# Three more scalings and one copy on ScalarE, one constant added by VectorE, wider weight sums, and a new instruction order in a Winograd residual block

## The chip, the cores and the metric

The kernel runs on one core of a Trainium2 chip. The metric is the device time of one execution in microseconds (us). A profile was taken of one execution; its time stands with the others below. The engines are called as in the profile: PE is TensorE (matmuls; PEld is its weight load), DVE is VectorE, ACT is ScalarE, POOL is GpSimd, SP is SyncE, which here only issues DMAs. Each engine runs its own instructions strictly in the order in which the program lists them and waits for the others by semaphores.

## The reference

Two images (`B = 2`) of 512 channels and 64 x 64 pixels in bf16 go through a residual block: group normalisation in four groups of 128 channels, silu, a 3 x 3 convolution of 512 to 512 channels, an embedding added per channel, and all of it once more:

```python
h = conv3(_silu(gn(x, g1, be1)), w1)
emb = _silu(t_emb) @ w_emb
h = h + emb.reshape(B, C, 1, 1)
h = conv3(_silu(gn(h, g2, be2)), w2)
return x + h
```

## The kernel before

**The arithmetic.** The convolution is done in Winograd form. A tile of rows is turned into combinations of rows (`v_block`, on DVE and ACT), the weights into the matching combinations (`u_blocks`, after transposes on PE), PE multiplies the two and accumulates over channels and taps, and the products are combined into output rows (`one_set`). The row form makes positions 0 to 5 out of four output rows. Positions 0 and 5, and in some chunks also 1 and 3, are computed with a second, column-wise form (`col_pair`, `more_cols`), which costs fewer matmuls and more work on DVE and ACT.

**Tiles and loops.** Channels stand on the 128 partitions, so there are four channel blocks `ct` in and four `ot` out. There are two layers and four chunks of 32 image rows (`chunks`, `idx` 0 to 3: image 0 upper and lower, image 1 upper and lower). For every layer, chunk and `ot`, `one_set` issues the matmuls of a set and the combining work. Between chunks, `v_block(layer, b, ch, c0, n, ...)` prepares a later chunk for two channel blocks at once (`n = 2`; one at a time for the very first chunk). The V buffers alternate between two chunks. The matmuls write three PSUM tiles `acc` in turn, and two more PSUM tiles `xa`, `xb` serve transposes and lone row positions; a tile is free for new matmuls when ACT or DVE has read it.

**Order.** Nothing is issued as the loops run. Every instruction is recorded in a plan (`plan.add`) with its engine, an assumed cost (`vcost` for DVE, `c` in `act`, `cost=` in `pool`) and what it reads and writes. `_Plan.issue` then runs a list scheduler on these costs, forwards and backwards, perturbs the priorities in stages with the random seeds of `STEPS` (L31 to L40), and emits the last order. `FIRST` (L30) is the assumed time to a DMA's first byte. So any change of a cost, of `FIRST` or of `STEPS` gives another order on all engines. All DVE additions go through `tt` (line L330 in the profile), scalings with a constant through `ts` (L335, with two constants L337), all ACT work but the transposes' copies (L531) and two others through `act` (L360).

**Places that the change touches.**
- `STEPS`, `FIRST` (L30 to L40), the assumed costs in `vcost` (L323), `act` (L350) and the power on POOL in `norm` (L458, L459).
- `norm`: mean and variance of a group become scale and shift. Where the statistics come through a PSUM tile (`ps`), DVE already adds epsilon; otherwise POOL adds it (L455) and then raises to the power -1/2 (L458).
- `u_more` (L487), once per `ot` and pair of channel blocks after chunk 0 of layer 1, makes the weights for the column form of positions 1 and 3: two DVE sums, a doubling `ts(g(1), g(1), 2.0)` on DVE (L493), and a third DVE sum.
- `v_block`: first a factor 4 (L658, by ACT in layer 1 and by DVE in layer 0, through `scaled`), then sums. For a chunk in column form, even and odd columns are pulled apart (L683 to L688): for chunks of `ACT_SPLIT` DVE adds in place and ACT makes the copy that pulls apart, for the others DVE adds and pulls apart in one instruction.
- `u_blocks`: six weight sums of 384 elements for each block of 128 input channels (L549 to L554), or, with `wide=True`, three sums of twice the size (L542 to L545), for which the middle tap goes to a scratch tile. Layer 1 uses the wide form with `tmp2`, the upper half of the tile `aux`; layer 0 uses the narrow one (L1071).

Of the kernel before, what the change touches and what calls it, by code (L numbers as in the profile page):

```python
# [11 lines left out]
ACT = mybir.ActivationFunctionType  # L12
ALU = mybir.AluOpType
# [11 lines left out]
class _Plan:  # L25
# [1 line left out]

    LOOK = {"PE": 0.0, "DVE": 0.25, "ACT": 0.6, "POOL": 0.0, "SP": 0.0}
    RATE = 0.36e6
    FIRST = 2.2  # L30
    STEPS = ((0, 3), (300001, 3), (300002, 3), (300003, 2), (300004, 3), (300006, 3), (300007, 3), (300008, 2),  # L31
# [9 lines left out]
    NOISE = 6.0  # L41

    def __init__(self):
# [149 lines left out]
def kernel(  # L193
# [13 lines left out]
    nc = tc.nc  # L207
# [15 lines left out]
    EPS = 1e-5  # L223
# [9 lines left out]
    DVE_SUMS = (1,)  # L233
    COL0 = (1, 2, 3)
    LONE = 1
    ACT_SPLIT = (1, 2, 3)
    MORE = 1
    DSTEP = (TR * P, CQ)
    SLOT = (1, 3, 2, 4, 0, 5)
    assert C % P == 0 and E % P == 0 and C // 4 == P and H % CR == 0 and NFREE == 512  # L240
# [40 lines left out]
    tmp2 = aux[:, CR * W:2 * CR * W]  # L281
# [25 lines left out]
    def size(a):  # L307
        n = 1
        for d in list(a.ap)[1:]:
            n *= d[1]  # L310
        return n
# [5 lines left out]
    def vcost(kind, aps):  # L317
        n = max(size(a) for a in aps)
        if n <= 16:
            return 0.08  # L320
        fast = all(packed(a) for a in aps)
        if kind == "tt":
            return 0.08 + n * (0.00051 if fast else 0.00102)  # L323
        if kind == "ts":
            return 0.07 + n * (0.00026 if fast else 0.00102)
        return 0.08 + n * 0.00104
# [5 lines left out]
    def ts(out, in_, c, op=ALU.mult, c2=None, op1=None, more=(), **kw):  # L332
        def emit():
            if op1 is None:
                nc.vector.tensor_scalar(out=out, in0=in_, scalar1=c, scalar2=None, op0=op)  # L335
            else:
                nc.vector.tensor_scalar(out=out, in0=in_, scalar1=c, scalar2=c2, op0=op, op1=op1)  # L337
        plan.add("DVE", vcost("ts", (out, in_)), emit, [in_] + list(more), [out], **kw)
# [8 lines left out]
    def act(out, in_, func=None, scale=1.0, bias=None, accum=None, **kw):  # L347
        fn = func or ACT.Copy
        ps = in_.tensor.name in psum
        c = size(in_) * (0.00093 if fn == ACT.Silu else 0.00081 if ps else 0.00084) + 0.09  # L350
        if accum is not None:
            c += 0.08

        def emit():
            extra = {}
            if bias is not None:
                extra["bias"] = bias
            if accum is not None:
                extra["accum_out"] = accum
            nc.scalar.activation(out=out, in_=in_, func=fn, scale=scale, **extra)  # L360
        reads = [in_] + [a for a in (scale, bias) if a is not None and not isinstance(a, float)]
        plan.add("ACT", kw.pop("cost", c), emit, reads, [out] + ([] if accum is None else [accum]), **kw)

    def scaled(out, in_, c, on_act):
        if on_act:
            act(out, in_, scale=c)
        else:
            ts(out, in_, c)
# [13 lines left out]
    def pool(emit, reads, writes, cost=0.45, **kw):  # L382
        plan.add("POOL", cost, emit, reads, writes, **kw)
# [23 lines left out]
    def norm(layer, b, c0, n, me, ps=None, quick=False):  # L407
        bank = None
        if ps is None:
            bank = XBank("xb", [2 * n], F32)  # L410
        tok = ["xb"] if ps is None else []

        def mm():
            o = ps if ps is not None else bank.get()[:]
            nc.tensor.matmul(o, lhsT=ones_neg[:], rhs=me[:], start=True, stop=True)
        plan.add("PE", 0.15, mm, [me[:], ones_neg[:]], tok if ps is None else [ps], lat=0.2, lead=100.0,
                 wait=0.05 if ps is not None else LATE)
        cols = 2 * n if ps is None else 3
        tot = small([cols], "tot")
        pin = tok if ps is None else [ps]  # L420

        def copy_tot():
            plan.add("DVE", 0.1, lambda: nc.vector.tensor_copy(out=tot[:], in_=ps if ps is not None else bank.get()[:]),
                     pin, [tot[:]])
        nvar, rstd = small([n], "nvar"), small([n], "rstd")
        mu, ex = tot[:, 0:n], tot[:, cols - n:cols]
        sc, nb = sc_all[layer, b][:, c0:c0 + n], nb_all[layer, b][:, c0:c0 + n]
        g_, b_ = gam(layer)[:, c0:c0 + n], bet(layer)[:, c0:c0 + n]

        def two(out, in0, in1, op, fast=False):  # L430
            if fast:
                tt(out, in0, in1, op)
            else:
                pool(lambda: nc.gpsimd.tensor_tensor(out=out, in0=in0, in1=in1, op=op), [in0, in1], [out])

        quick = quick or n == 1 or (layer, b) == (1, B - 1)
        if ps is not None:
            copy_tot()
            stt(nvar[:], mu, tot[:, 1:2], ex, ALU.mult, ALU.subtract)
        elif n == 1 and quick:  # L440
            copy_tot()
            stt(nvar[:], mu, mu, ex, ALU.mult, ALU.add)
        else:
            copy_tot()
            two(nvar[:], mu, mu, ALU.mult, quick)
            two(nvar[:], nvar[:], ex, ALU.add, quick)
        if ps is not None:
            ts(rstd[:], nvar[:], 0.0, op=ALU.max, c2=EPS, op1=ALU.add)
        elif quick:
            ts(nvar[:], nvar[:], 0.0, op=ALU.min, c2=-1.0, op1=ALU.mult)  # L450
        else:
            pool(lambda: nc.gpsimd.tensor_scalar(out=nvar[:], in0=nvar[:], scalar1=0.0, scalar2=-1.0,
                                                 op0=ALU.min, op1=ALU.mult), [nvar[:]], [nvar[:]])
        if ps is None:
            pool(lambda: nc.gpsimd.tensor_scalar(out=rstd[:], in0=nvar[:], scalar1=EPS, scalar2=None, op0=ALU.add),  # L455
                 [nvar[:]], [rstd[:]])
        nh = neg_half[:, 0:n]
        pool(lambda: nc.gpsimd.tensor_tensor(out=rstd[:], in0=rstd[:], in1=nh, op=ALU.pow), [rstd[:], nh], [rstd[:]],  # L458
             cost=0.9)  # L459
        two(sc, rstd[:], g_, ALU.mult, quick)  # L460
        if layer == 1:
            two(mu, mu, emb_sb[:, b, c0:c0 + n], ALU.add, quick)
        if n == 1 and quick:
            stt(nb, mu, sc, b_, ALU.mult, ALU.add)
        else:
            two(nb, mu, sc, ALU.mult, quick)
            two(nb, nb, b_, ALU.add, quick)
# [19 lines left out]
    def u_more(layer, ot, c0, n):  # L487
        U = u_pair(layer, ot, c0)
        g = lambda kx: slots(U, c0, n, S_UP + kx, [[2 * KP, 2], [1, P]])
        m = slots(U, c0, n, 1, [[S_G2 * P, 2], [1, P]])  # L490
        tt(m, g(0), g(2), ALU.add)
        tt(m, m, g(1), ALU.subtract)
        ts(g(1), g(1), 2.0)  # L493
        tt(g(1), g(1), m, ALU.add)

    def next_stage():
# [3 lines left out]
    def u_load(layer, ot, ct, **kw):  # L500
        wn = next_stage()
        dma(wn[:], w_v[layer][ot][:, ct * CQ:(ct + 1) * CQ], writes=[wn[:]], **kw)
        return wn
# [113 lines left out]
    def v_block(layer, b, ch, c0, n, Vs, res=None, on_act=(False, True, True), clean=False):  # L617
        idx = b * NCH + ch
# [20 lines left out]
        for c in range(n):  # L639
# [3 lines left out]
                scale=sc_all[layer, b][:, ct:ct + 1])  # L643
# [11 lines left out]
        R = src2 if n == 2 else src[half]  # L655
        rs = lambda j: view(R, j * TR * W, [[W, TR], [2 * TR * W, n], [1, W]])
        vv = lambda i: view(V, i * IN + (c0 % 2) * 2 * NI + 1, [[WP, 2 * TR], [2 * NI, n], [1, W]])
        scaled(q2, rows2(1), 4.0, layer == 1)  # L658
        tt(s2, rows2(3), rows2(1), ALU.subtract)
        tt(q2, q2, rows2(3), ALU.subtract)  # L660
        scaled(rs(0), r_, 0.25, on_act[1])
# [406 lines left out]
        v_block(0, 0, 1, c0, 2, Vbuf[2:4], res=xt, clean=True)  # L1068
    for ot in range(2, CT):
        for c0 in range(0, CT, 2):  # L1070
            u_blocks(0, ot, c0, [u_load(0, ot, c0), u_load(0, ot, c0 + 1)])  # L1071
    late = [sc_all[0, 0][:, CT - 1:CT]]
    load_parms(1, (g2, be2), late)
    plan.add("ACT", 0.1, lambda: nc.scalar.dma_start(out=tparm, in_=t_emb.rearrange("b (et p) -> (b et) p", p=P)),
# [98 lines left out]
```

## Time and profile before

| what | value |
|---|---|
| median of three runs | 488.69 us (487.36, 488.69, 589.78) |
| the profiled execution | 488.46 us |
| its span, first to last instruction | 486.6 us |
| mean granted TensorE clock | 0.999 |
| ACT busy | 398.0 us (82%), 510 instructions |
| POOL busy | 44.4 us (9%), 95 instructions |
| DMA | 55.55 MB, mean 114 GB/s |

The profiled execution took 1.9 us more than its span. "Busy" is the time covered by an engine's instructions; neighbouring instructions overlap in the records, for matmuls strongly, since they are pipelined and their ends are modelled. For PE the distance from one matmul's start to the next is therefore the better measure. Over the 3305 matmuls of the trace its median is 216 ns for 512 columns (1344 of them), 109 ns for 256 columns (1264) and 55 ns for 128 columns (509). The sum over all matmuls with the median of their width is 463.9 us; what single steps exceed their median by more than 40 ns sums to 13.1 us: 5.1 us before 20 us, 1.0 us from 20 to 60 us, 1.0 us from 60 to 120 us, 2.3 us from 120 to 300 us, 3.8 us after that. The first matmul starts at 1.06 us and the last ends at 481.9 us.

In the views below, "idle before" is the time in which an engine did nothing before an instruction, with the instruction that released it behind the arrow.

### The profile page before, as it was taken

How to read it: one execution, taken by the hardware profiler on the slowest of the kernel's cores; microseconds unless marked ns; L12 is line 12 of the kernel's file. 1: busy time of each engine (PE TensorE's matmuls, PEld its weight loads, DVE VectorE, ACT ScalarE, POOL GpSimd, SP SyncE). 2: the span in 40 equal slices, each digit the busy share in tenths (PEclk: the TensorE clock that was granted, in tenths of full speed). 3: DMA queues.
4: the chain of work that ended last, by engine and by line, in shares of the span. 5: the costliest groups of instructions: out<-in, count | busy, mean ns of one | idle time of the engine just before them, and what ended most of it. 6: DMA issues, size and time to landing. Idle time of an engine off the chain costs nothing. (4 is left out here: it accounts for less than half of the span.)

```text
span 486.6 us, 8586 instructions
## 1 busy us (share of the span) xinstructions
PE 474.2 (97%) x3305; PEld 294.3 (60%) x3305; DVE 456.1 (94%) x848; ACT 398.0 (82%) x510; POOL 44.4 (9%) x95
## 2 busy tenths in 40 slices
PE   7999999999999999999999999999999999999996
PEld 7855554455556555665665664557666686666774
DVE  2899899999999989799999999999999999999976
ACT  1799999999987869799999999958759397973653
POOL 3210000112220020000000000020001000000010
PEclk9999999999999999999999999999999999999999
DMA  8533223840013141315353212353633535533264
GB/s 308 189 95 98 92 85 130 270 163 17 29 44 128 49 126 56 109 49 181 113 157 99 94 44 89 86 171 94 172 90 88 150 70 158 148 88 86 45 174 131
DMA packets 17316, 55.55 MB, mean 114 GB/s; under 512 B 1915, under 2 KB 3067, under 8 KB 16507
## 3 DMA queue, kind: packets, MB, share of 16 engines
q1 hardware_dynamic: 14912, 46.86, 28.1%
q0 software_dynamic: 2160, 7.87, 9.7%
q8 instruction: 26, 0.43, 0.4%
q10 hardware_dynamic: 203, 0.27, 0.2%
q14 instruction: 15, 0.12, 0.1%
HBM read 38.22 MB, written 16.78 MB: 113 GB/s over the span
## 5 line engine op out<-in xcount | busy, mean ns | idle before, releaser
L719 PE MATMUL acc<-V,U 128*128 128x512 bf16 (+2 forms) x2096 | 363.3, 326 | 2.9 <-DVE V L330 1.0
L719 PEld LDWEIGHTS <-U 128*128 128x128 bf16 x2352 | 226.3, 98 | 146.2 <-issue 7.0
L330 DVE TENSOR_TENSOR V<-at 128x2048 bf16<-128x2048 bf16 (+2 forms) x68 | 67.1, 1003 | 2.3 <-ACT at L360 2.1
L360 ACT ACTIVATE m<-w 128x512 bf16<-128x512 bf16 x62 | 37.7, 631 | 18.5 <-DVE w L330 17.9
L360 ACT ACTIVATE at<-src,arena 128x2112 bf16<-128x2112 bf16 x20 | 43.6, 2207 | 7.8 <-DVE V L330 6.0
L330 DVE TENSOR_TENSOR w<-m,w 128x1024 bf16<-128x1024 bf16 (+1 forms) x63 | 42.9, 682 | 0.6
L750 PEld LDWEIGHTS <-U 128*128 128x128 bf16 x288 | 28.1, 97 | 24.2 <-issue 0.8
L360 ACT ACTIVATE mb<-acc 128x1024 bf16<-128x1024 f32 x36 | 36.6, 1017 | 7.3 <-DVE sd L330 5.4
L750 PE MATMUL xa<-V,U 128*128 128x512 bf16 x144 | 37.1, 381 | 0.3 <-ACT w L755 0.3
L750 PE MATMUL xb<-V,U 128*128 128x512 bf16 x144 | 37.3, 381 | 0.0
L330 DVE TENSOR_TENSOR U<-U 128x768 bf16<-128x768 bf16 (+3 forms) x72 | 35.1, 507 | 0.3
L531 ACT COPY U<-xa 128x768 bf16<-128x768 bf16 x31 | 25.0, 806 | 7.5 <-PE xa L399 7.5
L399 PEld LDWEIGHTS <-spare 128*128 128x128 bf16 x288 | 25.4, 143 | 9.0
L360 ACT ACTIVATE at<-V,arena 128x2112 bf16<-128x2112 bf16 x12 | 26.1, 2191 | 5.1 <-DVE arena L343 4.6
L330 DVE TENSOR_TENSOR sd<-mb 128x512 bf16<-128x512 bf16 x72 | 28.7, 417 | 0.2 <-ACT mb L360 0.2
L330 DVE TENSOR_TENSOR V<-V 128x2048 bf16<-128x2048 bf16 x24 | 28.9, 1222 | 0.0
L360 ACT ACTIVATE src<-V 128x1024 bf16<-128x1024 bf16 x24 | 24.9, 1052 | 0.7 <-DVE V L330 0.6
L360 ACT ACTIVATE m<-acc 128x1024 bf16<-128x1024 f32 x20 | 20.5, 1027 | 4.4 <-DVE y L330 3.4
L378 POOL DMA_DIRECT2D y<-in_x_dram x12 | 10.6, 887 | 142.1 <-DVE y L330 103.5
L360 ACT ACTIVATE aux<-V 128x2048 bf16<-128x2048 bf16 x12 | 22.9, 1909 | 0.6 <-DMA V<-in_x_dram 0.6
L360 ACT ACTIVATE w<-acc 128x1024 bf16<-128x1024 f32 x20 | 20.5, 1023 | 3.4 <-DVE y L330 2.5
L330 DVE TENSOR_TENSOR w<-w 128x1024 bf16<-128x1024 bf16 x31 | 21.2, 685 | 0.8
(152 smaller groups left out, 621.8 us busy)
## 6 DMA issues: line engine op xcount, KB each, us to landing
spare<-in_w_dram SPq DMA_DIRECT2D x32, 288.0 KB, 2.9
src<-h_scr SPq DMA_DIRECT2D x16, 528.0 KB, 4.7
V<-in_x_dram SPq DMA_DIRECT2D x6, 1024.0 KB, 8.6
y<-in_x_dram POOLq DMA_DIRECT2D x12, 512.0 KB, 5.5
out_dram<-y SPq DMA_DIRECT2D x12, 512.0 KB, 2.7
h_scr<-y SPq DMA_DIRECT2D x11, 512.0 KB, 2.6
h_scr<-aux SPq DMA_DIRECT2D x5, 512.0 KB, 8.0
src<-in_x_dram SPq DMA_DIRECT2D x4, 528.0 KB, 3.9
```

The lines of the kernel that those rows point to most:

```text
L330: lambda: nc.vector.tensor_tensor(out=out, in0=in0, in1=in1, op=op), [in0, in1], [out], **kw)
L360: nc.scalar.activation(out=out, in_=in_, func=fn, scale=scale, **extra)
L378: q.dma_start(out=out, in_=in_, **extra)
L399: nc.tensor.transpose(sel(t), in_, ident[:in_.shape[0], :in_.shape[0]])
L531: lambda: nc.scalar.copy(out=out, in_=sel(bank.get())), [tok], [out])
L719: nc.tensor.matmul(ap, lhsT=l, rhs=r, start=k == 0, stop=k == total[key] - 1)
L750: nc.tensor.matmul(bank.get()[:], lhsT=taps[i][0], rhs=taps[i][1], start=done[0] == 1, stop=done[0] == len(taps))
```

## The change

Six things change.

1. `ACT_SPLIT` also holds chunk 0: in layer 1's first chunk ACT pulls the columns apart.
2. The factor 4 of chunk `idx == 3` of layer 0 is taken by ACT as well.
3. The doubling in `u_more` moves from DVE to ACT.
4. In `norm`, epsilon is added by DVE instead of POOL where the small operations are DVE's anyway (`quick`).
5. `u_blocks` of layer 0's last two output blocks uses the wide form with `tmp2`.
6. Some assumed costs, `FIRST` and the seeds differ, and so the order on every engine.

```diff
-    FIRST = 2.2
-    STEPS = ((0, 3), (300001, 3), (300002, 3), (300003, 2), (300004, 3), (300006, 3), (300007, 3), (300008, 2),
...
+    FIRST = 3.0
+    STEPS = ((0, 3), (1100001, 3), (1100004, 3), (1100005, 3), (1100007, 3), (1100008, 2), (1100009, 2),
...
-    ACT_SPLIT = (1, 2, 3)
+    ACT_SPLIT = (0, 1, 2, 3)
     MORE = 1
+    POW = (0.6, 0.95, 1.9, 1.7)
...
-            return 0.08 + n * (0.00051 if fast else 0.00102)
+            return 0.08 + n * (0.00051 if fast else 0.00102) + (0.036 if n > 1536 else 0.0)
...
-        c = size(in_) * (0.00093 if fn == ACT.Silu else 0.00081 if ps else 0.00084) + 0.09
+        c = size(in_) * (0.00095 if fn == ACT.Silu else 0.00081 if ps else 0.00084) + 0.09
...
-            pool(lambda: nc.gpsimd.tensor_scalar(out=rstd[:], in0=nvar[:], scalar1=EPS, scalar2=None, op0=ALU.add),
-                 [nvar[:]], [rstd[:]])
+            if quick:
+                ts(rstd[:], nvar[:], EPS, op=ALU.add)
+            else:
+                pool(lambda: nc.gpsimd.tensor_scalar(out=rstd[:], in0=nvar[:], scalar1=EPS, scalar2=None, op0=ALU.add),
+                     [nvar[:]], [rstd[:]])
...
-             cost=0.9)
+             cost=POW[c0] if ps is not None else 0.9)
...
-        ts(g(1), g(1), 2.0)
+        act(g(1), g(1), scale=2.0)
...
-        scaled(q2, rows2(1), 4.0, layer == 1)
+        scaled(q2, rows2(1), 4.0, layer == 1 or idx == 3)
...
-            u_blocks(0, ot, c0, [u_load(0, ot, c0), u_load(0, ot, c0 + 1)])
+            u_blocks(0, ot, c0, [u_load(0, ot, c0), u_load(0, ot, c0 + 1)], tmp2, wide=True)
```

21 rows, old and new, of the table STEPS are left out of this document.

## The prediction

> **What bounds the kernel now.** First read the page's busy times and the 40 slices, then the table of stretches of 20 us, then PE's waits, then the chain that ended last.
>
> ```profile
> PE 474.2 (97%) x3305; PEld 294.3 (60%) x3305; DVE 456.1 (94%) x848; ACT 398.0 (82%) x510; POOL 44.4 (9%) x95
> ...
> DVE  2899899999999989799999999999999999999976
> ACT  1799999999987869799999999958759397973653
> ```
>
> PE is busy nearly throughout, and DVE is nine tenths full from 36 us almost to the end, so DVE's position decides where PE waits. ACT is full too until about 160 us and from 200 to 330 us; its room lies elsewhere.
>
> ```profile
> core 0: us, PE busy (x) PEld busy (x) DVE busy (x) ACT busy (x) POOL busy (x), PEclk, DMA share, GB/s
> ...
> 120.00:140.00 20.00, 19.81 (x117) 11.30 (x116) 19.81 (x41) 18.99 (x24) 6.31 (x8) 1.00 0.07 28
> 280.00:300.00 20.00, 20.00 (x125) 11.57 (x123) 20.00 (x37) 20.00 (x23) 0.00 (x0) 1.00 0.14 42
> 300.00:320.00 20.00, 19.83 (x116) 11.25 (x115) 20.00 (x35) 19.28 (x19) 1.98 (x2) 1.00 0.35 97
> 380.00:400.00 20.00, 19.22 (x148) 14.30 (x147) 19.89 (x32) 12.33 (x15) 1.72 (x2) 1.00 0.55 134
> ```
>
> The columns after the comma are busy us and counts. The granted clock is 1.00 throughout. From 280 to 320 us three engines are full at once (ACT 39.28 of 40 us); at 380 ACT has a third of its time free and PE loses 0.8 us while DVE is full.
>
> ```profile
> PE acc L719 <- DVE V L330: 1.0, 3, 0.5
> PE acc L719 <- ACT m L360: 0.8, 2, 0.5
> PE acc L719 <- ACT mb L360: 0.6, 2, 0.5
> ```
>
> These are PE's waits (us in total, times, longest). PE waits for DVE directly, or for ACT's evictions of `acc`. The second kind is DVE's too, since ACT's `m` scalings mostly stood idle before DVE's `w`:
>
> ```profile
> L360 ACT ACTIVATE m<-w 128x512 bf16<-128x512 bf16 x62 | 37.7, 631 | 18.5 <-DVE w L330 17.9 <-DVE arena L983 0.6
> ```
>
> All of it is small. The matmuls at the median distance of their width sum to 463.9 us; everything beyond is 13.1 us, 5.1 of it before 20 us. The single losses over 0.2 us after 200 us stand at 216, 251, 308, 340, 362, 383, 418 and 449 us and sum to 3.4 us; all that is lost between 200 and 449 us, small steps included, is 4.9 us. The chain that ended last is PE's until about 463 us, then DVE and ACT.
>
> **The sum, part by part.** The rows of the groups of one line and shape give the durations; behind the bar stand busy us and the mean of one in ns:
>
> ```profile
> L330 DVE TENSOR_TENSOR at<-src 128x2048 bf16<-128x2048 bf16 x8 | 18.3, 2290 | 0.2
> L330 DVE TENSOR_TENSOR src<-src 128x2048 bf16<-128x2048 bf16 x6 | 7.5, 1251 | 0.0
> L360 ACT ACTIVATE at<-src 128x2048 bf16<-128x2048 bf16 x6 | 12.2, 2038 | 1.7 <-DVE src L330 1.7
> L335 DVE TENSOR_SCALAR V<-at 128x2048 bf16<-128x2048 bf16 x6 | 4.2, 706 | 0.0
> L360 ACT ACTIVATE V<-at 128x2048 bf16<-128x2048 bf16 x8 | 15.3, 1907 | 0.0
> L335 DVE TENSOR_SCALAR U<-U 128x512 bf16<-128x512 bf16 x8 | 2.4, 302 | 0.0
> L330 DVE TENSOR_TENSOR U<-U 128x768 bf16<-128x768 bf16 x24 | 12.8, 552 | 0.2
> L330 DVE TENSOR_TENSOR U<-U 128x1536 bf16<-128x1536 bf16 x8 | 7.6, 948 | 0.0
> ```
>
> Two DVE additions of 417 ns back to back cover 0.75 us, so neighbours overlap by 0.084 us; for ACT two of 631 ns cover 1.15 us, an overlap of 0.11.
>
> 1. Chunk 0 in the split: two instructions of 2.290 become two of 1.251, DVE −2.08; ACT +2 x 2.038.
> 2. Factor 4 of layer 0's last chunk: two instructions, DVE −2 x (0.706 − 0.084) = −1.24; ACT +2 x 1.907.
> 3. Doubling: eight, DVE −8 x (0.302 − 0.084) = −1.74; ACT +8 x 0.631, taking the `m<-w` row of the same size.
> 4. Epsilon: POOL loses 4 x 0.760 + 0.45 = 3.5 us and is no bound at 44.4 us; DVE gets five instructions of 128x1, between 0 and 0.15 us each (the small rows beside them), taken at 0.07: +0.35. It also drops a change of engine in a chain that leads to the chunk's first scaled rows.
> 5. Wide sums: four blocks, 4 x (6 x 0.468 − 3 x 0.865) = 0.85 off DVE.
> 6. The order: the same instructions stand elsewhere on every engine.
>
> DVE: 2.08 + 1.24 + 1.74 + 0.85 − 0.35 = **5.6 us less** (with whole durations 7.0), 456.1 to about 450.5. ACT: 4.08 + 3.81 + 5.05 = 12.9, less 12 x 0.11, **11.6 us more**, 398.0 to 409.6. PE's 3305 matmuls stay.
>
> The Trainium skill, "ScalarE: Activation LUTs", section "Rules for kernel authors", speaks against parts 2 and 3: plain multiplications belong on VectorE, up to about 3x faster in bf16. The trace agrees (1907 against 706 ns); by that rule alone, counting engine time, ACT's 11.6 against DVE's 5.6 would make the edits a loss of 6 us.
>
> What lies beside other work? I took both orders, gave each instruction the duration of its row, and for every matmul took the PE time queued ahead of it minus the DVE time queued up to what it needs: the lead. The smallest per stretch goes from 6.2–7.4 to 5.4–6.7 us at 20–50 us, from 7.1–7.5 to 6.0–6.2 at 70–90, from 7.0–9.7 to 8.8–10.6 at 100–160, from 10.6–18 to 15.5–19 at 200–330, and from 7.1–12.1 to 13.4–16.7 at 330–440. So DVE comes 3 to 6 us earlier where the late waits are, and 0.7 to 1.3 us later early on. The same for ACT: from 24.5–31 to 17.0–20.6 at 280–330, where ACT is full. PE waited for ACT only where this lead was near 12 us, so 5 us of cover are left; that cover is what prices the 11.6 us on ACT at nothing.
>
> What is queued behind the moved work: on ACT, behind the doublings, which wait until PE has left the weights' tile and for two DVE sums, stand evictions of `acc` in layer 1, for which PE waits; six of the eight doublings stand near each other there. The split copies wait for DVE's addition, with `m` scalings behind them; the factor 4 only stands ahead of the same block's scalings. Each such wait is between 0 and one row (0.63 to 2.04 us); I take 0, since the doublings' inputs stand well ahead. On SP the store of chunk 0's first output block stands behind two weight loads of layer 0, and another store now ahead of layer 1's weights and of a load of x. Their landing rows are 2.9 us (weights) and 8.6 us (x), the room between release and first use is as large as before or larger (5 us became 8 for the tightest weights): 0, at most one landing. On POOL two edge memsets of 0.15 us move ahead of the powers of two channel blocks; they are ready earlier: 0. The wide sums share the upper half of `aux` with odd columns of the first chunk and with scrap outputs of the statistics: 0 to one instruction of 0.95 us in each block; 0 taken, the largest bound is in the rivals.
>
> By place:
> - 200–449 us: PE loses 4.9. The earlier DVE ends most waits, but a wait for a buffer or another engine stays; I take 70%: −3.4 (0 to −4.9).
> - 60–200 us: 1.9 lost, of which the early half keeps its lead: −0.5 (0 to −1).
> - before 20 us: another `FIRST`, other first instructions: +0.4 (0 to +0.8).
> - 20–60 us: leads down by about 0.7 us, 0.95 us of waits exist: +0.3 (0 to +1.1).
> - tail: the work after the last large group was 9.7 us on PE, balanced with 9.8 on DVE and ACT; the new order leaves PE 9.05 us and correspondingly ends later against DVE's unchanged chain: +0.65 (0 to +0.7).
>
> Net −2.55: 488.46 − 2.55 = **485.9 us**. The profiled time is 0.23 below the median 488.69, so against that it is −0.57%.
>
> **Rivals.**
> - *DVE is the bound itself, and all its relief comes through.* It is full for 440 us, and PE's 97% is drawn from overlapping matmuls with modelled ends, PEld is at 60%. Then 488.46 − 5.6 = 482.9, with the longer durations 481.5. Against it: PE's starts leave only 8.0 us of loss after 20 us, part of it too short to be a wait for an engine. The Trainium skill, "Perfetto Trace Analysis", section "Identifying the Most-Contended Engine", holds matmul busy time for a bad measure and looks at weight loads instead; by it DVE at 94% would be the bound, and the time the one of this rival; the trace's distances between matmuls, a measure which it doesn't use, speak against.
> - *Nothing left, or the order gives it back.* The late gain of 3.4 goes at the start, in 20–90 us (leads of 5.4 us), in a landing or in the tail: their upper bounds 0.8 + 1.1 + 0.7 = 2.6, and one landing of 2.9: 488.46 − 3.4 − 0.5 + 5.5 = 490.1. For it: before 90 us every lead falls.
> - *It doesn't do what it says.* The wide sums wait for `aux`, 4 x 0.95 = 3.8 us, eating more than their 0.85: 485.9 + 3.8 = 489.7.
> - *Slower: ACT becomes the pace.* ACT had 0.72 us free from 280 to 320 us and the moved work goes partly there; if its evictions come late, each `acc` tile is freed late and PE follows ACT. It decides when ACT's lead falls under 12 us, from 17 as ordered, so if ACT's real durations, or waits in its queue behind doublings, cost 5 us more than the rows. Then all 11.6 us may land on PE: 488.46 + 11.6 = 500.1. Against: ACT was idle for 17 us between 100 and 320 us.
>
> **How the numbers follow.** What can be told from no change here is about 2%, 9.8 us: below 478.9 or above 498.5 us. The forecast (483 to 488) gets 0.55, nothing left or given back (488 to 491) 0.26, the edit not doing what it says 0.05, DVE as the bound 0.10, ACT as the pace 0.04. The first four are within 2%, except that DVE's 7.0 us together with 4 us of other waits would give 477.5: 0.02 of its 0.10. So faster 0.02, same 0.94, slower 0.04. The range of 8 in 10 leaves out ACT as the pace and the outer half of DVE as the bound, and reaches to the end of the given-back case: 482.5 to 491.0. The forecast's own range is 483 to 488.
>
> **What would show it.** DVE's busy time near 450.5 and ACT's near 409.6 confirm the sum; the rows should show eight instead of six `at<-src` copies on ACT, ten instead of eight scalings `V<-at` of 128x2048 there, eight `U<-U` of 128x512 there at about 0.63 us, and 8 instead of 24 rows `U<-U` of 128x768 on DVE (the two others of a block also read another tile). The waits at 216 to 449 us should shrink from 4.9 to about 1.5 us; ACT should stand idle more often before DVE's results, not PE before ACT's. If PE's waits for `m`, `mb` or `acc` on ACT grow between 280 and 330 us, the fourth rival is right; if early waits (20 to 90 us) grow by more than 1.1 us, or PE starts its first convolution matmul well after 21.9 us, the second. The prediction is wrong in its base if the median distance between matmuls changes, since I hold that at 463.9 us.

## The result and the profile after

| | before | changed |
|---|---|---|
| median | 488.69 us | 484.16 us (483.50 to 484.48, five runs) |
| profiled execution | 488.46 us | 484.48 us |
| its span | 486.6 us | 482.6 us |

The ratio is 0.9903, 95% interval 0.9877 to 0.9929: about 1% faster, clear of its interval and below 2%. The forecast was 485.9 us and 0.57%. Repeated in the last experiment, the ratio was 0.9905 (0.9877 to 0.9933). One of the five executions of the kernel before took 589.78 us, far slower than the others, and is left out of the ratio.

First the page of the changed kernel: busy times and the slices of DVE and ACT.

```profile
PE 473.5 (98%) x3305; PEld 295.2 (61%) x3305; DVE 452.0 (94%) x831; ACT 407.8 (84%) x522; POOL 43.0 (9%) x90
...
DVE  2999999999999899998999999999999999999885
ACT  1699999999995989999999999978769497972663
```

DVE's busy time fell by 4.1 us and ACT's rose by 9.8. The shares hardly moved: a table of shares does not show why the kernel got faster. PE's waits do.

```profile
PE acc L1035 <- DVE ones_bf L1001: 1.1, 1, 1.1
PE acc L1059 <- DMA V<-in_x_dram: 1.0, 2, 0.7
PE acc L419 <- DVE acc L347: 0.7, 1, 0.7
PE acc L726 <- DVE U L334: 0.5, 1, 0.5
PE acc L726 <- DVE y L334: 0.3, 1, 0.3
```

The first three belong to the start. Of the list of before, the waits for ACT's `m` and `mb` and for DVE's `V` are gone from it; what is left in the convolutions (L726) is 0.8 us. In the stretches of 20 us (after the span's length: PE, PEld, DVE, ACT, POOL busy us and counts, clock, DMA share, GB/s) PE is busy as follows:

```profile
120.00:140.00 20.00, 20.00 (x119) 11.49 (x118) 19.86 (x49) 20.00 (x28) 4.07 (x5) 1.00 0.07 27
280.00:300.00 20.00, 20.00 (x134) 12.11 (x133) 20.00 (x34) 20.00 (x27) 1.11 (x1) 1.00 0.33 97
380.00:400.00 20.00, 19.65 (x142) 13.68 (x141) 19.72 (x31) 15.80 (x18) 1.06 (x2) 1.00 0.44 105
```

At 120 us PE is full where it lacked 0.19 us before. At 280 us it is full as before, beside a DVE and an ACT without a gap. At 380 us it lacks 0.35 us instead of 0.78.

The groups by line and shape confirm the edits (out<-in, count, then busy us, mean ns of one, and idle before):

```profile
L334 DVE TENSOR_TENSOR at<-src 128x2048 bf16<-128x2048 bf16 x6 | 13.7, 2285 | 0.0
L334 DVE TENSOR_TENSOR src<-src 128x2048 bf16<-128x2048 bf16 x8 | 10.0, 1254 | 0.7 <-ACT src L364 0.7
L364 ACT ACTIVATE at<-src 128x2048 bf16<-128x2048 bf16 x8 | 16.3, 2042 | 0.7 <-DVE V L334 0.5 <-DVE src L334 0.2
L364 ACT ACTIVATE V<-at 128x2048 bf16<-128x2048 bf16 x10 | 19.1, 1912 | 0.0
L364 ACT ACTIVATE U<-U 128x512 bf16<-128x512 bf16 x8 | 4.7, 670 | 1.0 <-DVE U L334 1.0
L334 DVE TENSOR_TENSOR U<-U 128x768 bf16<-128x768 bf16 x8 | 4.3, 552 | 0.1
L364 ACT ACTIVATE m<-w 128x512 bf16<-128x512 bf16 x62 | 38.3, 646 | 8.7 <-DVE w L334 8.6
```

The counts are those of the sum, and so are the durations, but for the doublings' 670 ns instead of 631 (see the last section). The last row tells more: ACT's `m` scalings stood idle for 17.9 us before DVE's `w`, now for 8.6. All of ACT's listed waits for DVE together went from 53 to 33 us. DVE's results come earlier, and ACT has filled part of the time that it stood idle.

For the places, the measure of the prediction is used again: for each two matmuls, the distance of their starts less the median of the width (216, 109, 55 ns), counted where it exceeds 40 ns. (For 128 columns the trace's median is 58 ns, not 55; this changes the first column by 0.3 us at most and the others not at all.) The losses in us, by time in the kernel's own span, here and below up to 500 us:

| kernel | 0–20 | 20–160 | 160–300 | 300–500 | after 20 us |
|---|---|---|---|---|---|
| before | 5.1 | 2.7 | 1.6 | 3.8 | 8.0 |
| changed | 5.3 | 1.1 | 0.0 | 2.5 | 3.6 |

From the end of the last matmul to the end of the span it was 4.7 us and is 5.1. So −4.4 after 20 us, +0.2 at the start, +0.4 at the tail make −3.8 of the span's −4.0.

### The profile page after: what moved, and what is told of

It reads as the page before. It is cut to its first block, busy times and chain, and to the rows that moved or that the text cites. A ratio compares the mean times of both kernels' runs of the same rounds, so it can differ in the third digit from the quotient of the medians.

```text
span 482.6 us, 8580 instructions
## 1 busy us (share of the span) xinstructions
PE 473.5 (98%) x3305; PEld 295.2 (61%) x3305; DVE 452.0 (94%) x831; ACT 407.8 (84%) x522; POOL 43.0 (9%) x90
## 5 line engine op out<-in xcount | busy, mean ns | idle before, releaser
L726 PE MATMUL acc<-V,U 128*128 128x512 bf16 (+2 forms) x2096 | 361.9, 326 | 1.0 <-DVE U L334 0.5
L726 PEld LDWEIGHTS <-U 128*128 128x128 bf16 x2352 | 226.1, 98 | 139.8 <-issue 1.9
L757 PE MATMUL xb<-V,U 128*128 128x512 bf16 x144 | 36.3, 381 | 0.0
L538 ACT COPY U<-xa 128x768 bf16<-128x768 bf16 x31 | 26.2, 846 | 7.6 <-PE xa L403 7.6
L334 DVE TENSOR_TENSOR U<-U 128x512 bf16<-128x512 bf16 (+3 forms) x60 | 30.8, 523 | 0.7 <-ACT U L364 0.5
L334 DVE TENSOR_TENSOR U<-U,aux 128x1536 bf16<-128x1536 bf16 x24 | 22.9, 953 | 0.5
L364 ACT ACTIVATE aux<-aux 128x768 bf16<-128x768 bf16 (+2 forms) x20 | 22.6, 1130 | 0.1
```

The lines of the kernel that those rows point to most:

```text
L334: lambda: nc.vector.tensor_tensor(out=out, in0=in0, in1=in1, op=op), [in0, in1], [out], **kw)
L538: lambda: nc.scalar.copy(out=out, in_=sel(bank.get())), [tok], [out])
L726: nc.tensor.matmul(ap, lhsT=l, rhs=r, start=k == 0, stop=k == total[key] - 1)
L757: nc.tensor.matmul(bank.get()[:], lhsT=taps[i][0], rhs=taps[i][1], start=done[0] == 1, stop=done[0] == len(taps))
```

## Experiments

Two theories. **Relief**: less work on DVE ended PE's waits, and ACT's new work fits into its idle time. **Order**: the new arrangement paid, and the edits matter little. A third, **ACT as the pace**, is the slower rival of the prediction. Since an edit that is planned anew also gets another order, most experiments freeze the order: an instruction is planned with the engine and cost of one kernel, but issued on the engine of the other, so everything else stands where it stood. The "four edits" below are the split of chunk 0, the factor 4, the doublings and epsilon; the wide sums stay with their order and are tested alone further down. Times are medians; intervals are of the ratio to the kernel before on the same chip.

### Edits and order, two by two

The four edits in the old order (for the split, the in-place sum and ACT's copy are issued at the old instruction's place; epsilon likewise):

```diff
-        ts(g(1), g(1), 2.0)
+        plan.add("DVE", vcost("ts", (g(1), g(1))), lambda o=g(1): nc.scalar.activation(
+            out=o, in_=o, func=ACT.Copy, scale=2.0), [g(1)], [g(1)])
...
+            plan.add("DVE", vcost("ts", (q2, rows2(1))), lambda: nc.scalar.activation(
+                out=q2, in_=rows2(1), func=ACT.Copy, scale=4.0), [rows2(1)], [q2])
```

> Every instruction stands where it stood before; the doubling, the factor 4 of layer 0's last chunk, the copy of chunk 0 and epsilon only change their engine in place (the wide sums are left out). DVE is relieved by 4.75 us, ACT gets 11.6 us. Relief theory: the late waits for DVE end as they do in the changed kernel, 3 of its 4.0 us come, about 485.5 us, ratio 0.993. Order theory: the edits alone are worth nothing and only the new order pays, 488 to 489 us. ACT theory: the 11.6 us come in the way in an order that was not made for them, above 491 us.

The same edits undone in the new order:

```diff
-        act(g(1), g(1), scale=2.0)
+        plan.add("ACT", size(g(1)) * 0.00084 + 0.09, lambda o=g(1): nc.vector.tensor_scalar(
+            out=o, in0=o, scalar1=2.0, scalar2=None, op0=ALU.mult), [g(1)], [g(1)])
```

> Every instruction stands where the changed kernel has it, but the same four edits are undone in place (the wide sums stay). DVE gets 4.75 us back. Relief theory: the late waits for DVE come back, 487.5 to 489 us, ratio near 1. Order theory: it stays at the changed kernel's 484 to 485 us, ratio 0.992.

| | old order | new order |
|---|---|---|
| without the four edits | 489.15 us (the kernel before) | 490.45 us, ratio 1.0032 (1.0015 to 1.0050) |
| with them | 500.7 us, 1.0225 (1.0192 to 1.0258) | 484.16 us, 0.9903 (0.9877 to 0.9929) |

In the old order only the ACT theory's expectation (above 491 us) holds. In the new order the relief theory has the direction and too small a size (487.5 to 489 us), and the order theory fails. The same edits lose 2.25% in one order and gain 1.3% in the other (0.9903 over 1.0032, each against the kernel before). Neither the new order nor the edits gain anything alone. Undoing them reopens PE's waits for DVE, directly and through ACT's `m`, whose scalings `m<-w` then stand idle for 16.3 us before DVE's `w`; this is the list of waits after 150 us with the edits undone in the new order (in the changed kernel it holds the two last lines of the list above):

```profile
PE acc L736 <- DVE y L347: 2.3, 2, 1.4
PE acc L736 <- ACT m L364: 1.8, 2, 1.2
PE acc L736 <- DVE U L334: 1.0, 1, 1.0
PE acc L736 <- DVE y L334: 0.6, 2, 0.4
```

In the old order with the edits the longest waits, but for the DMAs of x at the start, are for ACT; `mb` had cost 0.6 us before:

```profile
PE acc L734 <- ACT mb L360: 4.5, 4, 2.2
PE acc L1067 <- DMA V<-in_x_dram: 2.3, 3, 1.2
PE xb L399 <- ACT aux L533: 1.7, 1, 1.7
PE xa L399 <- ACT U L533: 1.5, 2, 1.1
PE xa L765 <- ACT w L770: 1.2, 1, 1.2
```

One place shows how this comes about. The timelines give start, duration, engine, line and operation, and in brackets the idle time before. The kernel before, around the factor 4 of layer 0's last chunk:

```profile
166.29 0.70 DVE L335 TENSOR_SCALAR V<-at 128x2048 bf16<-128x2048 bf16 x1
...
167.03 1.26 DVE L330 TENSOR_TENSOR V<-V,at 128x2048 bf16<-128x2048 bf16 x1
...
171.90 1.00 ACT L360 ACTIVATE mb<-acc 128x1024 bf16<-128x1024 f32 x1
...
172.95 0.81 PE L719 MATMUL acc<-V,U 128*128 128x512 bf16 x3 [0.17 <-ACT mb L360]
```

And with the edits in that order:

```profile
169.79 1.90 ACT L661 ACTIVATE V<-at 128x2048 bf16<-128x2048 bf16 x1
...
171.72 1.26 DVE L330 TENSOR_TENSOR V<-V,at 128x2048 bf16<-128x2048 bf16 x1 [2.66 <-ACT V L661]
...
176.59 1.00 ACT L360 ACTIVATE mb<-acc 128x1024 bf16<-128x1024 f32 x1
...
177.64 0.81 PE L734 MATMUL acc<-V,U 128*128 128x512 bf16 x3 [2.17 <-ACT mb L360]
```

ACT takes the factor after an eviction, DVE's next instruction stands waiting for it for 2.66 us, all that DVE does afterwards comes later, so does the eviction `mb`, and PE waits 2.17 us for its `acc` where it had waited 0.17. In the changed kernel two other DVE instructions, both `w<-m,w`, stand between the factor and the sum that needs it, and the sum doesn't wait; there PE waits for nothing between 160 and 300 us:

```profile
164.40 1.91 ACT L364 ACTIVATE V<-at 128x2048 bf16<-128x2048 bf16 x1
164.98 1.41 DVE L334 TENSOR_TENSOR w<-m,w 128x1024 bf16<-128x1024 bf16 x2
...
166.33 1.26 DVE L334 TENSOR_TENSOR V<-V,at 128x2048 bf16<-128x2048 bf16 x1
```

To part ACT's new work from DVE's relief, the old order once more, with the moved work left out:

```diff
-        plan.add("DVE", vcost("ts", (g(1), g(1))), lambda o=g(1): nc.scalar.activation(
-            out=o, in_=o, func=ACT.Copy, scale=2.0), [g(1)], [g(1)])
+        plan.add("DVE", vcost("ts", (g(1), g(1))), lambda o=g(1): None, [g(1)], [g(1)])
...
-                    nc.scalar.activation(out=sp, in_=apart(w05 + 1, WP), func=ACT.Copy, scale=1.0)
```

> The first experiment again (old order, edits in place), but what ACT was given is left out of the computation: the doublings, the factor 4 of layer 0's last chunk and the copies of chunk 0 are done by no engine. DVE has its 4.75 us of relief and ACT no more than before. If ACT's moved work cost the first experiment its time, PE's losses after 20 us fall from 17.8 us to under 6 us and the time to 485 to 487 us. If the old order can't use DVE's relief either, they stay above the 8.0 us of the kernel before, 489 us or more.

Measured: 486.25 us, ratio 0.9961 (0.9939 to 0.9982), as expected if ACT's moved work was the cost. PE's waits behind the start are then DVE's alone, and small:

```profile
PE acc L731 <- DVE V L330: 1.0, 3, 0.5
PE acc L415 <- DVE arena L330: 0.6, 1, 0.6
PE acc L731 <- DVE arena L330: 0.4, 1, 0.4
PE acc L731 <- DVE y L330: 0.4, 2, 0.2
```

PE's losses, as above:

| kernel | 0–20 | 20–160 | 160–300 | 300–500 | after 20 us |
|---|---|---|---|---|---|
| old order, edits in place | 7.6 | 2.8 | 8.5 | 6.5 | 17.8 |
| old order, moved work left out | 5.5 | 2.5 | 0.0 | 3.0 | 5.5 |
| new order, edits undone | 4.9 | 1.1 | 4.2 | 4.3 | 9.5 |

Read by columns: from 20 to 160 us the loss goes by the order (2.5 to 2.8 in the old, 1.1 in the new, whatever the edits). After 160 us it goes by both: the edits take 8.4 to 2.5 us in the new order and 5.3 to 15.0 in the old. DVE's relief alone is worth 8.03 − 5.46 = 2.6 us in the old order. ACT's moved work costs 17.83 − 5.46 = 12.4 us there, close to the 11.2 us by which it lengthens ACT's busy time (408.4 us with it, 397.2 without).

That doesn't mean that ACT had no time for it. From 160 to 240 us, where PE lost 5.4 us, ACT was busy for 70.0 of 80 us, as in the kernel before (70.0); in the changed kernel it was busy for 76.7 us there, and PE lost nothing. DVE's busy time fell from 73.3 to 67.6 us in the same stretch, since DVE stood waiting for ACT. From 240 to 300 us ACT was full in all three kernels (59.0, 59.2 and 59.9 of 60 us), and only with the edits in the old order did PE lose 3.1 us. So a full ACT doesn't decide it; the place of the moved work does, as in the timeline above. Leaving the work out removes its time and its waits together, so this experiment alone can't part the two.

### Other seeds

Does any other order serve as well?

```diff
-    FIRST = 2.2
-    STEPS = ((0, 3), (300001, 3), (300002, 3),
...
+    FIRST = 3.0
+    STEPS = ((0, 3), (1100001, 3), (1100004, 3),
...
```

> The kernel before with the changed kernel's FIRST and STEPS, so another order of the same work. Relief theory: DVE's work is as before, so 488 to 490 us. Order theory: 484 to 486 us.

> The changed kernel with FIRST and STEPS of before: all edits, planned anew with other seeds. Relief theory: 485 to 486.5 us, since the relief is there under any good order. Order theory: 488 us or more.

The kernel before with the new seeds took 514.68 us (ratio 1.0524, 1.0500 to 1.0547), the changed kernel with the old ones 503.5 us (1.0296, 1.0276 to 1.0317). Both theories expected far less. PE's losses from 20 to 500 us are 29.6 and 21.4 us. Of these, 5.8 and 1.6 us lie in stretches in which the granted clock was 0.50 (last section), so that part is a slower clock and no wait; whether the order brings it about is not shown (all six executions of the kernel before with the new seeds had a mean granted clock of 0.972 to 0.984). For the rest the code suggests a reason, which was not tested: each step shifts the priorities that the steps ahead of it left, for the costs and instructions of its own kernel. Carried to other work the seeds are then a random disturbance. "A good order" can't be assumed to be there with any list of seeds. One rival stays open: the new list has 89 steps and the old one 73, and the kernel before was not given a list of its own of that length.

### The parts, each undone in the new order

> The changed kernel, every instruction in its place, only the eight doublings back on DVE. All four parts undone in place cost 6.3 us for 4.75 us of DVE. Relief theory: 1.74 us more on DVE between 313 and 353 us cost PE 1.3 to 2.3 us there and nothing before, 486 us. Rival (the doublings are covered on either engine): 484 to 484.5 us.

> Only the factor 4 of layer 0's last chunk back on DVE, in place (at 164 and 184 us). Relief theory: 1.24 us more on DVE, of which the losses of PE between 180 and 260 us take 0.8 to 1.6 us, 485.5 us. Rival (two instructions of 0.7 us are absorbed by DVE's lead): no change, 484.2 us.

The factor's edit is the mirror of the one above; for the split, the sum is left to the copy's place:

```diff
-            tt(w, w, view(R, 0, [[W, rows], [1, W]]), ALU.add)
-            act(sp, apart(w05 + 1, WP))
+            half = view(R, 0, [[W, rows], [1, W]])
+            plan.add("DVE", vcost("tt", (w, w, half)), lambda: idx == 0 or nc.vector.tensor_tensor(
+                out=w, in0=w, in1=half, op=ALU.add), [w, half], [w])
+            plan.add("ACT", size(sp) * 0.00084 + 0.09, lambda: nc.vector.tensor_tensor(
+                out=sp, in0=apart(w05 + 1, WP), in1=apart(0, W), op=ALU.add) if idx == 0 else nc.scalar.activation(
+                out=sp, in_=apart(w05 + 1, WP), func=ACT.Copy, scale=1.0), [apart(w05 + 1, WP)], [sp])
```

> Only the two copies of layer 1's first chunk back on DVE, in place (at 209 and 241 us). Relief theory: 2.08 us more on DVE and PE's losses at 209 to 260 us 2 to 3 us, 486.5 us, the largest part. Rival (the late waits come from the doublings alone): under 485 us.

```diff
-                ts(rstd[:], nvar[:], EPS, op=ALU.add)
+                plan.add("DVE", vcost("ts", (rstd[:], nvar[:])), lambda: nc.gpsimd.tensor_scalar(
+                    out=rstd[:], in0=nvar[:], scalar1=EPS, scalar2=None, op0=ALU.add), [nvar[:]], [rstd[:]])
```

> Only epsilon back on POOL, in place. By the sum DVE loses 0.35 us of work, so a gain of 0 to 0.35 us if it is throughput; if the change of engine in the chain to the first scaled rows counts, five POOL instructions of 0.45 to 0.76 us come into chains that PE waits for at the start: 0.5 to 2 us slower, all of it before 30 us.

For the wide sums each instruction of the wide form is issued as two halves:

```diff
-            tt(a, a, mh, ALU.add)
+                    for k in range(n):
+                        nc.vector.tensor_tensor(out=o[:, k], in0=i0[:, k], in1=i1[:, k], op=op)
```

> The changed kernel in its order, the wide weight sums of layer 0's last two output blocks issued as two sums of half the size each, 24 instructions in place of 12: DVE 0.85 us more, all before 200 us, where PE loses almost nothing. Throughput alone (as with the factor 4, where 1.24 us gave 1.0): 0.7 us slower, 485 us. Covered by idle time of DVE before 240 us: 484.2 us.

| undone | us | ratio to before | DVE busy, against 452.0 | PE's loss after 20 us, against 3.6 |
|---|---|---|---|---|
| doublings | 486.31 | 0.9951 (0.9935 to 0.9967) | +1.7 | 5.2: +1.4 at 300–350 |
| factor 4 | 485.69 | 0.9935 (0.9917 to 0.9953) | +1.2 | 4.6: +1.0 at 200–240 |
| split of chunk 0 | 488.02 | 0.9992 (0.9974 to 1.0010) | +1.7 | 6.7: +1.4 at 200–240, +1.7 at 240–300 |
| epsilon | 485.06 | 0.9925 (0.9905 to 0.9945) | −0.4 | 3.8 |
| wide sums | 485.02 | 0.9937 (0.9915 to 0.9960) | +0.4 | 3.7 |

The losses after 20 us stand where the undone instructions stand or soon after, and they add up: 1.6 + 1.0 + 3.1 + 0.2 = 5.9, which is what all four undone together cost (9.5 − 3.6). The changed kernel's nine executions all had a mean granted clock of 0.998 or more; the others' medians also hold executions at 0.990 to 0.997. Without those the medians are 485.9, 485.4, 487.6, 485.0 and 484.7 us in the order of the table, against 483.9. The relief theory holds for doublings and factor 4 as expected, and the split is the largest part, as expected, but cost more than DVE's busy time says. Its timeline shows the reason:

```profile
208.70 2.29 DVE L695 TENSOR_TENSOR at<-src 128x2048 bf16<-128x2048 bf16 x1
210.90 0.68 DVE L334 TENSOR_TENSOR w<-m,w 128x1024 bf16<-128x1024 bf16 x1
...
211.62 0.63 ACT L364 ACTIVATE m<-w 128x512 bf16<-128x512 bf16 x1 [3.82 <-DVE w L334]
...
216.81 4.52 PE L730 MATMUL acc<-V,U 128*128 128x256 bf16 x28 [1.23 <-ACT m L364]
```

The long sum stands ahead of DVE's `w`, ACT idles 3.82 us for that, and PE then waits 1.23 us. (In the frozen order the sum stands at the copy's place; planned anew it might stand better, which wasn't tried.) For the factor 4 the interval of the ratio overlaps the changed kernel's; what shows its part is the loss of 1.0 us at 200 to 240 us, where the changed kernel loses nothing. For epsilon and the wide sums nothing beyond the noise is shown: their losses after 20 us differ by 0.1 to 0.2 us from the changed kernel's, and the intervals overlap its own.

### How much more ACT could take

```diff
-        act(g(1), g(1), scale=2.0)
+        def emit(o=g(1)):
+            nc.scalar.activation(out=o, in_=o, func=ACT.Copy, scale=2.0)
+            nc.scalar.activation(out=o, in_=o, func=ACT.Copy, scale=1.0)
+        plan.add("ACT", size(g(1)) * 0.00084 + 0.09, emit, [g(1)], [g(1)])
```

> The changed kernel, every instruction in its place, each doubling followed by a copy of the same size onto itself on ACT: 8 x 0.55 = 4.4 us more for ACT between 312 and 348 us, nothing more for DVE. Forecast's cover (ACT's lead of 17 us, PE waits under 12): PE's losses there grow by less than 0.7 us, 484 to 485 us. ACT as the pace: most of the 4.4 us arrive, 487 us or more.

> The changed kernel once more, on the same chip as these: 484.2 us, ratio 0.990, PE's losses after 20 us 3.6 us.

The changed kernel took 483.89 us again (losses after 20 us 3.6), the one with each doubling twice 485.68 us, 0.9951 (0.9933 to 0.9969). By PE's losses neither expectation holds: the loss from 300 to 350 us grew from 1.1 to 2.1 us, a quarter of the 4.4 us. The timeline has it in one wait:

```profile
318.40 0.63 ACT L502 ACTIVATE U<-U 128x512 bf16<-128x512 bf16 x1
318.94 1.01 ACT L364 ACTIVATE w<-acc 128x1024 bf16<-128x1024 f32 x1
...
319.99 8.23 PE L729 MATMUL acc<-V,U 128*128 128x256 bf16 x45 [1.45 <-ACT w L364]
```

The eviction `w<-acc` stands behind the first four doublings. In the changed kernel it began 2.80 us after the first of them (312.93 to 315.73 us), now 4.85 us (314.09 to 318.94). Of the 2.05 us that it is later by that measure, PE waits 1.45 us: the cover at this place is about 0.6 us, not the five that the forecast read from the leads. The losses after 20 us explain 1.2 us of the 1.8 us between the medians. The rest is not the doubled doublings' work: in this run's profile the granted clock was 0.50 from 10.2 to 13.6 us, where PE lost 1.5 us, and the five of its twelve executions with a mean of 0.998 or more have a median of 484.6 us, 0.7 us above the changed kernel's.

## Why the prediction came out

It was right in sign and range, with somewhat over half the size, and not by every step. Two errors partly cancelled: the late gain was forecast 0.9 us too large, the gain before 200 us 1.7 us too small. That the sum came so near is in part luck.

- **The base** holds: the matmuls' nominal sum is 463.7 us after 463.9, and the time went by PE's losses.
- **DVE's relief** was summed to 5.6 us; the page shows 4.1. With the order frozen, the four edits move 3.8 to 3.9 us instead of 4.75 (455.8 against 452.0 in the new order, 456.1 against 452.2 in the old with the moved work left out; 452.9 with it on ACT). Doublings and factor 4 measured as forecast (1.7 and 1.2); the split gave 1.7 instead of 2.08, the wide sums 0.4 instead of 0.85.
- **ACT's load**, forecast 11.6, is 11.1 to 11.2 with the order frozen.
- **200 to 449 us**: forecast −3.4 of 4.9, measured 4.9 to 2.4, −2.5. The losses left there stand at 300 to 400 us. (The prediction's list of single losses lacks one, 0.7 us at 384 us, in PE's wait for DVE's `V`; its 4.9 us include it.)
- **20 to 200 us** is where a step failed, the reading of the leads. At 20 to 60 us they fell by about 0.7 us and +0.3 was charged for it; measured was −0.5 (0.95 to 0.47). For 60 to 200 us −0.5 was forecast, at most −1; measured was −1.4 (2.1 to 0.6). Both lie outside their own bounds. From 20 to 160 us this part is the order's and not the four edits': the loss is 1.1 us with them and without them in the new order, 2.7 and 2.8 in the old; nor is it the wide sums', for with these undone it is 1.2. Why the smallest lead misjudged the order was not tested; it adds up durations and leaves out waits between DVE and ACT, and that is the likely reason.
- **Start and tail**: +0.4 and +0.65 forecast, +0.2 and +0.4 measured; the start is within what it varies by.
- **Taking the edits one by one at cost nothing on ACT** was right only for this order. The rival "ACT becomes the pace" gave 500.1 us, all 11.6 us on PE's path; in the old order the edits took 500.7 us. The numbers agree, the mechanism only in part: ACT's evictions did come late, but because DVE waited for moved work in a bad place, not because ACT was full. In the new order the rival did not happen; but the lead of ACT on which its chance of 0.04 rested overstated the room, as the doubled doublings show.
- **One of its signs was wrong**: ACT was to stand idle more often before DVE's results. It did so less (53 to 33 us); what came true beside it is that PE's waits for ACT's `m` and `mb` went.
- **DVE as the bound** (481.5 to 482.9 us) did not come. PE's gain in the new order, 5.9 us for 3.8 us of DVE's time, is more than throughput explains: the waits run over two engines (`at<-src`, then `w`, then `m`, then PE), and one long instruction ahead of a short urgent one costs PE more than its own excess. The Trainium skill, "Perfetto Trace Analysis", section "Identifying the Most-Contended Engine", would optimize the engine of highest occupancy first and judges PE by its weight loads and its share of peak instead. By DVE's 94% beside 60% of weight loads that engine was DVE here (the share of peak was not worked out), and relieving it paid, but by single places, which occupancy does not show: 94% before and after.
- The rule of the Trainium skill, "ScalarE: Activation LUTs", section "Rules for kernel authors", that multiplications belong on VectorE, agrees in duration again (1912 ns against 704). By it the edits should lose. They do in the old order and win in the new; engine time alone does not decide it.

## What to carry to other kernels

Work moved from a full engine to one with idle time paid here only where its result was not the next thing that someone waited for, and where it did not hold up an eviction that frees PSUM. So judge such a move together with the order that it gets: freeze the order and swap the engine to see what the edit does, leave the moved work out to see what its new place costs. When an order comes from a search on assumed costs, treat its seeds as part of that one version: carried over, they made both kernels slower here. And before two profiles are compared by what PE lost, compare the granted clock in the same stretches.

## What was not expected of the hardware

- **The start varies, and the granted clock has a part in it.** The kernels with the doublings, the factor 4 or the split undone share all of their first 150 us, and yet PE lost 7.1, 6.6 and 4.7 us before 20 us. PE's wait for the DMAs of x was 2.2, 1.9 and 1.6 us in them, and 1.0 and 2.0 in the two profiles of the changed kernel. In the first two the granted clock was 0.50 for 3.4 us (9.5 to 12.9 and 8.8 to 12.2 us), in which PE lost 1.4 and 1.3 us; in the third it was 1.00 throughout the start. Differences of a us between single profiles mean little unless the first 20 us are taken out.
- **At a granted clock of 0.50 matmuls start at twice the distance.** In the kernel before with the new seeds it was 0.50 from 96.6 to 103.4 us, and there the median distance for 512 columns was 425 ns instead of 216. The mean over an execution shows such stretches: on the last chip the kernel before took 488.0 us (median of 16 executions) at a mean of 0.998 or more, and 489.4 us (8 executions) at 0.996 or less. What sets off such a stretch is not shown.
- **ACT's rows get longer where it never waits, without getting slower.** In the changed kernel the first doublings lasted 718 ns in the records, at 326 us one lasted 630; but they began at 312.93, 313.45, 313.97 and 314.49 us, 0.52 us apart. Where ACT runs back to back for long, neighbouring records overlap by 0.2 us and not by the 0.11 of the forecast's pair, so its cost is read from the distance of starts. The cause is not shown.
